# Two turns through the heads: weight slots that change contents in place of a ring of streamed pieces

## The chip, the core and the metric

The kernel runs on one core of a Trainium2 chip. The core has five engines with an instruction stream each: TensorE (PE; the profile shows its weight loads apart, as PEld), VectorE (DVE), ScalarE (ACT), GpSimd (POOL) and SyncE (SP), which here does nothing but issue DMAs. Sixteen DMA engines move data between DRAM and the on-chip memory SBUF. An engine takes its instructions in order, so an instruction that waits holds all behind it.

The metric is the time of one execution on the device, in microseconds: the median of three runs.

## The reference

Two independent models read their own inputs; their outputs are laid side by side. Part A is a dilated sliding-window attention. The change doesn't touch it except for copies that are made meanwhile. Part B is a recurrent memory transformer over 64 segments of 32 rows:

```python
# x: (1, 2048, 640), mem0: (1, 8, 640); 32 heads of 192; Wq, Wk, Wv: (640, 32, 192), Wo: (32, 192, 640)
mem = mem0
for s in range(64):
    h = concat([mem, x[:, 32 * s:32 * s + 32]], axis=1)          # 40 rows: 8 of memory, 32 of the segment
    q, k, v = h @ Wq, h @ Wk, h @ Wv                             # per head
    p = softmax(mask(q @ k.T * scale))
    o = (p @ v) @ Wo                                             # summed over the heads
    mem = o[:, :8]
    outs.append(o[:, 8:])
```

Each segment needs the memory of the one before, so the segments come one after the other, and each uses all four weights: 60 pieces of 384 KB for q, k and v, and 24 of 320 KB for the output, 31.5 MB in all. SBUF doesn't hold them all.

## The kernel before

**Part A** runs first (`part_a`, lines 24 to 265). Meanwhile SP loads weights of part B that fit beside it, then copies the weights that won't stay in SBUF to DRAM buffers in the layout in which they are fetched (`copy_streamed`), and issues the fourth x transpose (`turn_x(3)`) after these copies.

**A segment of part B.** The heads are taken in four groups of eight. Weight pieces have names (matrix, group, part): five for each group of q, k and v, six of output weights for each group. For each group a segment makes q, k and v (`project32`, matmuls of line 562 in PSUM tiles `acc`), moves them to SBUF and turns them, makes scores (line 626), a softmax, turns the probabilities (line 665), mixes the values (line 689, steps `mix` and `ot`) and multiplies with output weights: for the first three groups `project_out` (line 714, into Y), for the last one `project_last` (line 740). `close` adds the parts, writes the new memory into HX, the left operand of the next projections (line 748), and the output rows into XS (line 749).

The 40 rows of a segment are split: the main block of HX holds the 8 rows of memory and the first 24 x rows; the last 8 x rows of four segments stand together in a second block and are multiplied at once, ahead of their use (for the groups that table `RENEW` names for a segment; for q, one group at the end of each segment, step `ql`), and the results are kept in small blocks. The mixed values of these last 8 rows (the "late rows") are collected in DRAM (`late_o`, written by POOL's DMA, line 699) and multiplied with the output weights at the very end (`project_late`, line 859), four segments to a block.

**The order** is written out by hand as a list of steps, `ORDER` (`FIRST` for segment 0), and PE, DVE, ACT and SP follow it as written. The steps that matter here, in their order (a number is the group):

```python
q.0 k.0 k.1 q.1 v.0 q.2 k.2 v.1 q.3 k.3 out.0.0 v.2 out.0.1 v.3 PT.2 ve.2 ... out.1.1 out.2.0 out.2.1 part tx PT.3 mix.3 ot.3 last join ql close
```

`out.0.0` takes the first four output pieces of the group, `out.0.1` the other two. At `ve.2` SP is given the load of the next segment's x rows into XS (`load_x`, line 535), and at `tx` DVE turns these into HX (`turn_x`, line 531 from XS). The stores of the segment before (line 772, four of 7.5 KB) are given to SP at `tp.0`, `PT.0`, `tp.1` and `e.k3`.

**Weights.** 61 of the 84 pieces stay in SBUF (`wres_...`). The other 23, named in `STREAMED`, are fetched in each segment, in the order in which they are used, into a ring of seven slots (tile `t`, `fetch`, line 475): a fetch waits until PE has read the piece that was seven fetches earlier. SP issues them in the order of the program, and so runs seven slots ahead of PE. At the end, `project_late` goes through the output weights twice, for two blocks of rows at a time, with its resident pieces first and with the five streamed ones fetched again; the late rows are loaded into the dead q slots meanwhile (`load_late`).

Of the kernel before, what the change touches and what calls it, by code (L numbers as in the profile page):

```python
# [23 lines left out]
def part_a(ctx, tc, A_x, A_wqkv, A_wo, out, ident, emit_loads):  # L24
# [241 lines left out]
    with tc.manual_schedule(engines={mybir.EngineType.PE, mybir.EngineType.DVE, mybir.EngineType.Activation}):  # L266
# [4 lines left out]
        for b in range(-1, n_blk):  # L271
# [13 lines left out]
STREAMED = {"q": ((), (), (), ()), "k": ((1, 3), (1, 2), (0, 2), (1, 3)), "v": ((0, 1, 4), (2, 4), (0, 2, 4), (0, 2)),  # L285
            "o": (8, 12, 17, 19, 23)}
PARTS = {}
SLOT = 1536
# [18 lines left out]
SPREAD = "SSVV"  # L307
STORE_AT = ("tp.0", "PT.0", "tp.1", "e.k3")
LEAD_IN = 114
HEAD = 10  # L310
# [9 lines left out]
def part_b(ctx, tc, B_x, B_mem0, B_Wq, B_Wk, B_Wv, B_Wo, out, ident, n_seg, pre, nbuf, mid):  # L320
# [8 lines left out]

    def streamed(u):  # L330
        return u[1] in STREAMED["o"] if u[0] == "o" else u[2] in STREAMED[u[0]][u[1]]

# [15 lines left out]
    def quarter_cols(u):  # L348
        return 320 if u[0] == "o" else 384

    def load_quarters(dst, u, which):
        n = quarter_cols(u)
        for k, i in enumerate(which):
            to = dst[:, n * k:n * k + n]
            if u[0] == "o":
                src = unit_src(u)[:, i // 2].rearrange("p (b g c) -> p g b c", b=2, g=2)[:, i % 2]
                nc.sync.dma_start(to.rearrange("p (b c) -> p b c", b=2), src)
            else:
                nc.sync.dma_start(to, unit_src(u)[:, n * i:n * i + n])

    def quarter(w, u, i):

        n = quarter_cols(u)
        if isinstance(w, tuple):
            now = PARTS[u]
            v = w[0][:, n * i:n * i + n] if i < now else w[1][:, n * (i - now):n * (i - now) + n]
            return v.rearrange("p (b c) -> p b c", b=2) if u[0] == "o" else v
        if u[0] == "o":
            return w[:, 640 * (i // 2):640 * (i // 2) + 640].rearrange("p (b g c) -> p g b c", b=2, g=2)[:, i % 2]
        return w[:, n * i:n * i + n]  # L370

    def stream_cols(u):
        return quarter_cols(u) * PARTS.get(u, 4)

    def kept_cols(u):
        return quarter_cols(u) * (4 - PARTS[u]) if u in PARTS else unit_cols(u)

    copied = {}

    def copy_streamed():  # L380

        for m, g in need:
            for u in pieces(m, g):
                if u in PARTS:
                    copied[u] = dpool.tile([128, stream_cols(u)], BF16, name="wcopy_%s%d_%d" % u)[:]
                    load_quarters(copied[u], u, range(PARTS[u]))
                elif streamed(u):
                    copied[u] = dpool.tile([128, unit_cols(u)], BF16, name="wcopy_%s%d_%d" % u)[:]
                    nc.sync.dma_start(two_rows(copied[u], u), unit_src(u))

    need = [(m, g) for m, g in (("q", 0), ("k", 0), ("q", 1), ("k", 1), ("q", 2), ("k", 2), ("v", 0), ("v", 1), ("o", 0),
                                ("q", 3), ("k", 3), ("v", 2), ("o", 1), ("v", 3), ("o", 2), ("o", 3))]
    resident = []
    for m, g in need:
        resident += [u for u in pieces(m, g) if not streamed(u) or u in PARTS]
    res, wait = {}, set()

    def place_resident(pool, units):
        for u in units:
            res[u] = pool.tile([128, kept_cols(u)], BF16, name="wres_%s%d_%d" % u)[:]  # L400

    def load_resident(units):
        for u in units:
            if u in PARTS:
                load_quarters(res[u], u, range(PARTS[u], 4))
            else:
                nc.sync.dma_start(two_rows(res[u], u), unit_src(u))

    n_pre, used = 0, 0
    while n_pre < len(resident) and used < pre:  # L410
        used += 2 * kept_cols(resident[n_pre])
        n_pre += 1
# [28 lines left out]
    def emit_loads(turn_x):  # L441
        turn_x(1)
        load_resident(resident[:n_pre])
        turn_x(2)
        copy_streamed()
        return copy_windows
# [9 lines left out]
    wstream = pool("b_ws", bufs=nbuf)  # L456
    early = resident[n_pre:n_pre + 9]
# [13 lines left out]
    fetched = {}  # L471

    def fetch(u):
        t = wstream.tile([128, SLOT], BF16, tag="ws")
        nc.sync.dma_start(t[:, 0:stream_cols(u)], copied[u])
        return t[:, 0:stream_cols(u)]

# [7 lines left out]
    def get_unit(u):  # L485
        if u in wait:
            load_pending(u)
        if not streamed(u):
            return res[u]
        if u in fetched:  # L490
            w = fetched.pop(u)
        else:
            w = fetch(u)
            if pending:
                load_pending(pending[0])
        return (w, res[u]) if u in PARTS else w
# [155 lines left out]
    def put_p(s, g, t1, sm):  # L652
        i = s % 4
        if g == 0 and s:
# [14 lines left out]
    def spread_p(g, pt):  # L669
        PT = one.tile([128, 4, 2, L], BF16, tag="PT")  # L670
        if SPREAD[g] == "S":
# [34 lines left out]
    def project_out(Y, g, pairs=range(6)):  # L706
        for a in pairs:
            i = 6 * g + a
            w = get_unit(("o", i, 0))
            for r in range(2):  # L710
                c = 2 * a + r
                for gv in range(2):
                    t = 32 * (2 * r + gv)
                    nc.tensor.matmul(Y[t:t + 32].rearrange("p (b c) -> p b c", b=2),  # L714
                                     lhsT=OT[:, slot(c), 0:32], rhs=quarter(w, ("o", i, 0), 2 * r + gv),
                                     start=(i == 0), stop=(i == 17), tile_position=(0, t))
# [17 lines left out]
    def project_last(Y):  # L734
        for a in range(6):
            w = get_unit(("o", 18 + a, 0))
            for r in range(2):
                c = 2 * a + r
                for j in range(4):
                    nc.tensor.matmul(Y[32 * j:32 * j + 32], lhsT=OT[:, slot(c), 0:32],  # L740
                                     rhs=quarter(w, ("o", 18 + a, 0), 2 * r + j % 2)[:, j // 2],
# [16 lines left out]
    def segment(s):  # L758
# [9 lines left out]

        def step(name, *at):
            g = int(at[0][-1]) if at else None  # L770
            if ".".join((name,) + at) in STORE_AT and stores:
                nc.sync.dma_start(*stores.pop(0))
            if name in "qkv":
                project(name, g)
            elif name == "e":
                m = at[0][0]
                got["sb", m, g] = evacuate(m, got.pop((m, g)), [engine[c] for c in EVACUATE[at[0]]])
            elif name == "T":
# [3 lines left out]
                if m + at[0][1] == "k0" and s and keep:  # L782
# [17 lines left out]
            elif name == "PT":  # L800
                got["PT", g] = spread_p(g, got.pop(("p", g)))
            elif name == "ve":
                keep_values(g, got.pop(("v", g)))
                if g == 2:
                    load_x(s + 1)
            elif name == "mix":
                got["mix", g] = mix(g, got.pop(("PT", g)))
            elif name == "ot":
                keep_mix(s, g, got.pop(("mix", g)), [engine[c] for c in HEADS[g]])
            elif name == "out":  # L810
                g, half = int(at[0]), int(at[1])
                if "Y" not in got:
                    got["Y"] = ps_y.tile([128, 320], FP32, tag="y", name="Y")
                project_out(got["Y"], g, range(4 * half, 4 + 2 * half))
# [11 lines left out]
            elif name == "last":  # L826
                got["Z"] = bank()[:, 0:160]
                project_last(got["Z"])
# [10 lines left out]
    DEAD = [("q", g, dc) for g in range(4) for dc in range(5)]  # L839
# [4 lines left out]

    def project_late():

        O = [res[DEAD[b]].rearrange("p (g n c) -> p g n c", g=4, c=12) for b in range(16)]
        acc = [ps_acc.tile([128, 384], FP32, tag="acc", name=f"acc{n}") for n in range(3)]
        y = ps_y.tile([128, 320], FP32, tag="y")
        sums = [bank()[:] for _ in range(4)] + [acc[0][:], acc[1][:], acc[2][:], y[:]]  # L850
        head = [i for i in range(24) if not streamed(("o", i, 0))][:HEAD]
        tail = [i for i in range(24) if i not in head]

        def add(m, i, w, first, final):
            for r in range(2):
                c = (2 * i + r) % 12
                for gv in range(2):
                    for j in range(4):
# [3 lines left out]
                                         start=first and r == 0, stop=final and r == 1, tile_position=(0, 32 * j))  # L862
# [10 lines left out]
        for a, b in ((0, 1), (2, 3)):  # L873
            first = b == 1
            if first:
                load_late(range(8))
            for i in head:
# [110 lines left out]
```

## Time and profile before

| | us |
|---|---|
| median of three runs | 1859.13 (1856.05 to 1865.02) |
| the profiled execution, first to last instruction | 1879.4 |
| of it: start to line 748 of segment 0 | 207.8 |
| from there to line 748 of segment 62 | 1580.1 |
| last segment, up to the late products | 27.6 |
| late products and last stores | 63.9 |

The page of a profile gives the busy time of each engine over the span, the same in 40 slices of time, the DMA queues, the chain of work that ended last, and the costliest groups of instructions. "A <- B" behind an idle time means that B ended the wait of A. A line number is that of the kernel. PE's matmuls are pipelined and their ends modelled, so PE can be shown as busy while it runs below its peak. The names of DMAs are destination<-source: `t<-wcopy_v` is a fetch of a v piece into the ring, `wres_q<-in_B_Wq_dram` a load of a resident piece.

### The profile page before, as it was taken

How to read it: one execution, taken by the hardware profiler on the slowest of the kernel's cores; microseconds unless marked ns; L12 is line 12 of the kernel's file. 1: busy time of each engine (PE TensorE's matmuls, PEld its weight loads, DVE VectorE, ACT ScalarE, POOL GpSimd, SP SyncE). 2: the span in 40 equal slices, each digit the busy share in tenths (PEclk: the TensorE clock that was granted, in tenths of full speed). 3: DMA queues.
4: the chain of work that ended last, by engine and by line, in shares of the span. 5: the costliest groups of instructions: out<-in, count | busy, mean ns of one | idle time of the engine just before them, and what ended most of it. 6: DMA issues, size and time to landing. Idle time of an engine off the chain costs nothing.

```text
span 1879.4 us, 91426 instructions
## 1 busy us (share of the span) xinstructions
PE 1649.8 (88%) x39286; PEld 1048.1 (56%) x39286; DVE 1289.2 (69%) x3671; ACT 683.4 (36%) x1821; POOL 552.1 (29%) x1612
## 2 busy tenths in 40 slices
PE   8898888988888988988898889988888888889888
PEld 5565555555545555555555555555555555555568
DVE  4786776777666767767767767776677767777740
ACT  4454333333333333333333333333333333334320
POOL 3001322333322333323323323333333332333220
PEclk9999999999999999999999999999999999999999
DMA  9927999999999999999999999999999999999991
GB/s 327 319 72 258 368 356 335 362 365 362 350 340 328 351 330 368 355 360 352 357 341 367 345 345 361 366 364 339 354 355 354 348 338 356 348 355 371 331 373 36
DMA packets 277859, 627.63 MB, mean 334 GB/s; under 512 B 64116, under 2 KB 76898, under 8 KB 277452
## 3 DMA queue, kind: packets, MB, share of 16 engines
q1 hardware_dynamic: 267020, 610.59, 91.4%
q0 software_dynamic: 10336, 11.12, 1.7%
q8 instruction: 308, 5.05, 1.1%
q14 instruction: 99, 0.81, 0.1%
q10 hardware_dynamic: 96, 0.06, 0.0%
HBM read 607.47 MB, written 22.91 MB: 335 GB/s over the span
## 4 chain that ended last, share of the span: by engine, by line
PE 52%; DMA 25%; DVE 11%; issue 6%; ACT 4%; SPq 1%; POOL 0%; ACTq 0%; DVEq 0%; POOLq 0%
PE acc L562 27%; DMA t<-wcopy_v 19%; PE Y L714 6%; DMA t<-wcopy_k 4%; PE px L626 4%; PE px L689 3%; PE px L740 3%; PE pq L95 3%; PE px L859 2%; PE px L665 1%; DVE prod L151 1%; ACT OT L697 1%; DVE OT L697 1%; PE po L161 1%; ACT QT L721 1%
## 5 line engine op out<-in xcount | busy, mean ns | idle before, releaser
L562 PEld LDWEIGHTS <-HX 128*32 128x32 bf16 x19380 | 506.1, 97 | 373.4 <-issue 147.8
L562 PE MATMUL acc<-t,HX 128*32 128x384 bf16 x5812 | 432.5, 329 | 51.7 <-DMA t<-wcopy_v 34.8
L562 PE MATMUL acc<-wres_q,HX 128*32 128x384 bf16 x6460 | 328.4, 331 | 15.9 <-issue 14.0
L562 PE MATMUL acc<-wres_k,HX 128*32 128x384 bf16 x3876 | 271.3, 327 | 12.7 <-issue 10.6
L698 POOL COPY OL<-OT 128x96 bf16<-128x96 bf16 x256 | 159.4, 623 | 272.5 <-ACT OT L697 170.4
L562 PE MATMUL acc<-wres_v,HX 128*32 128x384 bf16 x3232 | 215.4, 328 | 7.9 <-issue 7.9
L697 DVE CAST OT<-px 128x240 bf16<-128x240 f32 x256 | 103.6, 405 | 168.4 <-PE px L689 153.0
L608 POOL COPY QT<-Lb 128x96 bf16<-128x96 bf16 x252 | 68.2, 271 | 482.5 <-PE px L626 482.1
L714 PE MATMUL Y<-wres_o,OT 128*32 128x320 bf16 x3840 | 193.0, 305 | 8.3 <-issue 8.3
L572 DVE STREAM_TRANSPOSE QT<-QT 128x384 bf16<-128x384 bf16 x256 | 146.6, 573 | 44.6 <-ACT QT L601 42.3
L601 ACT CAST KT<-acc 128x384 bf16<-128x384 f32 x192 | 92.4, 481 | 225.3 <-PE px L626 176.5
L697 ACT CAST OT<-px 128x240 bf16<-128x240 f32 x256 | 92.5, 361 | 217.5 <-PE px L689 123.7
L626 PE MATMUL px<-KT,QT 64*64 64x40 bf16 (+1 forms) x4096 | 138.7, 189 | 33.3 <-DVE KT L572 24.4
L615 ACT CAST Vst<-acc 128x384 bf16<-128x384 f32 x256 | 123.5, 483 | 118.1 <-PE px L689 94.0
L699 POOL DMA_DIRECT2D late_o<-OL x256 | 138.5, 541 | 77.0 <-POOL OL L698 60.8
L626 PEld LDWEIGHTS <-QT 64*64 64x64 bf16 (+1 forms) x4096 | 108.7, 109 | 90.8 <-issue 52.6
L632 DVE SCALAR_TENSOR_TENSOR px<-px,mask 128x160 f32<-128x160 f32 x256 | 82.7, 323 | 108.0 <-PE px L626 107.8
L714 PEld LDWEIGHTS <-OT 128*32 128x32 bf16 x4608 | 115.2, 97 | 62.4 <-issue 13.7
L572 DVE STREAM_TRANSPOSE KT<-KT 128x384 bf16<-128x384 bf16 x256 | 142.3, 556 | 3.3 <-ACT KT L601 1.7
L568 ACT CAST sb<-acc 128x384 bf16<-128x384 f32 x115 | 55.1, 479 | 236.3 <-PE acc L562 208.1
L689 PE MATMUL px<-PT,Vst 64*128 64x80 bf16 (+1 forms) x2048 | 123.5, 213 | 10.0 <-issue 6.3
L644 ACT ACTIVATE px<-px 128x160 f32<-128x160 f32 x256 | 74.2, 290 | 145.1 <-DVE px L643 137.0
(102 smaller groups left out, 2437.4 us busy)
## 6 DMA issues: line engine op xcount, KB each, us to landing
t<-wcopy_v SPq DMA_DIRECT2D x640, 384.0 KB, 5.7
t<-wcopy_k SPq DMA_DIRECT2D x512, 384.0 KB, 5.4
t<-wcopy_o SPq DMA_DIRECT2D x330, 320.0 KB, 5.9
wres_q<-in_B_Wq_dram SPq DMA_DIRECT2D x20, 384.0 KB, 7.8
late_o<-OL POOLq DMA_DIRECT2D x256, 24.0 KB, 5.2
wres_q<-late_o SPq DMA_DIRECT2D x16, 384.0 KB, 7.3
wres_o<-in_B_Wo_dram SPq DMA_DIRECT2D x19, 320.0 KB, 7.7
wres_k<-in_B_Wk_dram SPq DMA_DIRECT2D x12, 384.0 KB, 7.8
```

Source lines behind the costliest of these rows:

```text
L562: nc.tensor.matmul(ps[n][32 * j:32 * j + 32].rearrange("p (f n) -> p f n", n=32), lhsT=X[:, dc, :], rhs=columns(w, (m, g, dc), j), start=( ...
L572: nc.vector.transpose(t, t)
L601: copies[1](columns_of(m, 0, 32), ps[-1][:].rearrange("p (f n) -> p f n", n=32))
L615: S_(Vst[:], ps[-1][:])
L626: nc.tensor.matmul(Sps[64 * h:64 * h + 64, a, :], lhsT=QT[k0:k1, L * f:L * f + 64], rhs=KT[k0:k1, f, :], start=(outer == 0 and a == 0), st ...
L632: nc.vector.scalar_tensor_tensor(out=Sps, in0=Sps, scalar=scale, in1=mask[:].unsqueeze(1).to_broadcast([128, 4, L]), op0=ALU.mult, op1=ALU ...
L644: nc.scalar.activation(t1[:], t1[:], ACTF.Exp)
L689: nc.tensor.matmul(ps[r][lo:hi, 2 * L * k:2 * L * k + 2 * L], lhsT=V[64 * r:64 * r + 64, col:col + hi - lo], rhs=PT[64 * r:64 * r + 64, 2 ...
L697: copy(OT[:, 6 * r:6 * r + 6].rearrange("p c n -> p (c n)"), ps[r][:, 0:6 * L])
L698: nc.gpsimd.tensor_copy(OL[:, g % 2].rearrange("p n c -> p c n"), OT[:, :, 32:L])
L699: nc.gpsimd.dma_start(late_o[s // 4][:, g, s % 4], OL[:, g % 2].rearrange("p n c -> p (n c)"))
L714: nc.tensor.matmul(Y[t:t + 32].rearrange("p (b c) -> p b c", b=2), lhsT=OT[:, slot(c), 0:32], rhs=quarter(w, ("o", i, 0), 2 * r + gv), sta ...
```

## The change

The ring goes, and `STREAMED` with it. In its place:

- Odd segments take the groups in the order 3, 2, 1, 0 (`TURN`); even ones as before. The steps of `ORDER` now name positions, and the group is looked up. Tables of engines (`HEADS`, `SPREAD`, `EVACUATE`) go by position.
- Groups 0 and 3 of k, v and the output weights share slots (`SHARED`). When the group at position 0 has been used, its pieces are replaced by those of the other outer group (`change`, at k.0, v.0 and out.0.1), which is used at position 3 and, because the order turns, at position 0 of the next segment.
- One more slot holds pieces k1.4 and o17 in turn (`PAIR`): each is replaced by the other once it has been used.
- All of these are copied to DRAM during part A: 34 pieces (`copy_shared`) instead of 23.
- The load of XS remains at the step `ve` of position 2, and so follows the six output loads of `out.0.1` in SP's order.
- In the last segment the late rows, blocks 0 to 14, are loaded into the q slots as these fall free (at q of positions 0 to 2), and after v of position 1 the output pieces of group 0 go into slots of k and v (`load_outputs`), while the output pieces of group 3 stay. So all 24 are resident for `last` and for `project_late`, which takes one block of rows after the other through all weights.

```diff
+TURN = (0, 1, 2, 3), (3, 2, 1, 0)
+SHARED = (0, 3)
+PAIR = ("k", 1, 4), ("o", 17, 0)
...
+    def copy_shared():
+        for u in [u for g in SHARED[::-1] for m in "kvo" for u in pieces(m, g)] + list(PAIR):
+            copied[u] = dpool.tile([128, unit_cols(u)], BF16, name="wcopy_%s%d_%d" % u)[:]
+            nc.sync.dma_start(two_rows(copied[u], u), unit_src(u))
...
+    def replace(old, new):
+        slots[new] = slots.pop(old)
+        del res[old]
+        res[new] = slots[new][:, 0:unit_cols(new)]
+        nc.sync.dma_start(res[new], copied[new])
+
+    def change(m, g):
+        for old, new in zip(pieces(m, g), pieces(m, SHARED[0] + SHARED[1] - g)):
+            replace(old, new)
...
-    wstream = pool("b_ws", bufs=nbuf)
-    early = resident[n_pre:n_pre + 9]
+    early = resident[n_pre:n_pre + 16]
...
+        turn = TURN[s % 2]
+
         def step(name, *at):
-            g = int(at[0][-1]) if at else None
             if ".".join((name,) + at) in STORE_AT and stores:
                 nc.sync.dma_start(*stores.pop(0))
+            n = int(at[0][-1]) if at else None
+            g = turn[n] if at else None
             if name in "qkv":
                 project(name, g)
+                if name != "q" and n == 0:
+                    change(name, g)
+                if (name, g) == PAIR[0][0:2]:
+                    replace(*PAIR)
+                if s == 0 and n == 0 and name != "q":
+                    load_all("o", 1 if name == "k" else 2)
+                if last and name == "q" and n < 3:
+                    load_late(range(5 * n, 5 * n + 5))
+                if last and name == "v" and n == 1:
+                    load_outputs()
...
             elif name == "ve":
                 keep_values(g, got.pop(("v", g)))
-                if g == 2:
+                if n == 2:
                     load_x(s + 1)
...
+                project_out(got["Y"], g, range(4 * half, 4 + 2 * half), n == 0, n == 2)
+                if half and n == 0 and not last:
+                    change("o", g)
+                if half and g == PAIR[1][1] // 6 and not last:
+                    replace(*PAIR[::-1])
...
+    def load_outputs():
+        for old, new in zip(pieces("k", end[1]) + pieces("v", end[1]), pieces("o", end[3])):
+            replace(old, new)
...
     def project_late():
+        load_late((15,))
...
+        for m in range(4):
+            for i in range(24):
+                add(m, i)
+            store(m)
```

More of the change, by code (lines that the diff above doesn't have):

```diff
@@ L372, in stream_cols @@
[L372 to L376, printed above, removed]
-    copied = {}
[L380 to L389, printed above, removed]
@@ L487, in get_unit @@
             load_pending(u)
[L488 to L496, printed above, removed]
+        return res[u]
     mask = cpool.tile([128, L], BF16)
@@ L837, in segment @@
             step(*token.split("."))
-    DEAD = [("q", g, dc) for g in range(4) for dc in range(5)]
+    end = TURN[(n_seg - 1) % 2]
+    DEAD = [u for g in end for u in pieces("q", g)]
     def load_late(quads):
@@ L849, in project_late, with add @@
         y = ps_y.tile([128, 320], FP32, tag="y")
[L850 to L854, printed above, removed]
+        sums = [acc[0][:], acc[1][:], acc[2][:], y[:]] + [bank()[:] for _ in range(4)]
+        def add(m, i):
+            w = get_unit(("o", i, 0))
             for r in range(2):
```

128 lines of the change are left out of this document (35 added, 93 removed).

## The prediction

> **What bounds the kernel now.** I read the page first: busy times, DMA row, chain, DMA issues.
>
> ```profile
> span 1879.4 us, 91426 instructions
> ...
> PE 1649.8 (88%) x39286; PEld 1048.1 (56%) x39286; DVE 1289.2 (69%) x3671; ACT 683.4 (36%) x1821; POOL 552.1 (29%) x1612
> ...
> DMA  9927999999999999999999999999999999999991
> ...
> PE 52%; DMA 25%; DVE 11%; issue 6%; ACT 4%; SPq 1%; POOL 0%; ACTq 0%; DVEq 0%; POOLq 0%
> ...
> t<-wcopy_v SPq DMA_DIRECT2D x640, 384.0 KB, 5.7
> t<-wcopy_k SPq DMA_DIRECT2D x512, 384.0 KB, 5.4
> t<-wcopy_o SPq DMA_DIRECT2D x330, 320.0 KB, 5.9
> ```
>
> From a quarter of part A on, the DMA row stays at 9, and a quarter of the chain is DMA. The streamed pieces (`t`) are 10 v, 8 k and 5 o per segment: 18 x 393,216 + 5 x 327,680 bytes = 8.72 MB. Next the stages, from windows (columns: span; busy of PE, PEld, DVE, ACT, POOL; PE clock; DMA share; GB/s). The edges are line 748, which writes the recurrent memory into HX: once per segment, except the last.
>
> ```profile
> 0.00:170.00 170.00, 149.73 (x1971) 96.30 (x1972) 121.63 (x127) 81.65 (x159) 27.85 (x66) 0.99 0.75 236
> ...
> 207.80:1787.90 1580.10, 1388.08 (x34468) 864.30 (x34472) 1125.89 (x3426) 576.61 (x1595) 503.02 (x1488) 0.99 0.99 352
> 1787.90:1815.50 27.60, 22.82 (x551) 13.92 (x539) 17.46 (x52) 9.38 (x26) 9.31 (x26) 0.97 1.00 370
> 1815.50:1879.40 63.90, 55.37 (x1533) 52.65 (x1533) 1.97 (x4) 1.71 (x4) 1.32 (x3) 0.93 0.35 125
> ```
>
> 1580.1 us hold 62 segments: 25.49 us each. 8.72 MB at 352 GB/s are 24.8 us, and stores and x rows come on top: DMA sets the pace. What PE's waits say of the same stretch:
>
> ```profile
> PE acc L562 <- issue: 34.6, 49, 2.2
> PE acc L562 <- DMA t<-wcopy_v: 33.5, 62, 1.6
> ...
> PE px L689 <- issue: 10.0, 13, 1.3
> PE Y L714 <- issue: 8.7, 10, 2.8
> PE px L626 <- issue: 7.4, 14, 1.6
> PE px L740 <- issue: 5.3, 8, 1.3
> ...
> PE acc L562 <- DMA t<-wcopy_k: 3.9, 9, 0.7
> ...
> PE Y L714 <- DMA t<-wcopy_o: 1.1, 2, 0.6
> ```
>
> Weights: 38.5 us; "issue" (a sequencer with nothing to run): 66.0 us. The shortest segment of all shows how fast PE's own order can go (timeline):
>
> ```profile
> 1278.48 0.20 DVE L748 TENSOR_TENSOR HX<-Vst,KT 128x40 bf16<-128x40 f32 x1
> ...
> 1279.61 0.33 PE L562 MATMUL acc<-wres_k,HX 128*32 128x384 bf16 x4
> ...
> 1290.78 0.32 SPq L535 DMA_DIRECT2D XS<-xwindows  x1
> 1291.37 3.98 SPq L475 DMA_DIRECT2D t<-wcopy_o  x5
> ...
> 1292.12 0.73 PE L714 MATMUL Y<-wres_o,OT 128*32 128x320 bf16 x16
> ...
> 1293.69 0.46 PE L714 MATMUL Y<-wres_o,OT 128*32 128x320 bf16 x8
> ...
> 1298.01 0.35 DVE L531 STREAM_TRANSPOSE HX<-XS 128x160 bf16<-128x160 bf16 x1
> ...
> 1301.67 0.20 DVE L748 TENSOR_TENSOR HX<-Vst,KT 128x40 bf16<-128x40 f32 x1
> ```
>
> 23.2 us. Three marks count below: k's first piece is read 1.13 us after line 748 and done 0.33 later; the second part of the first output group is read at 15.2; line 531 turns the next segment's x rows (`tx`) at 19.5, and from there PT.3, mix.3, `last` and `close` take 3.66 to the next line 748.
>
> **The change, part by part.** *Traffic.* A segment now loads 5 k, 5 v and 6 o pieces (the other outer group's), plus o17 and k1.4 in turn: 11 x 393,216 + 7 x 327,680 = 6.62 MB, 24% less, 18.8 us at 352. The weight waits (38.5 us) go: a k piece is asked for at group 0 and used at group 3, some 10 us later.
>
> *What is late next: the x rows.* The load into XS stands behind `ve` of the third group in SP's order. Before, SP had run seven ring slots ahead and issued it at 12.3 us of the segment above, 7.2 ahead of `tx`. Now six o loads stand in front of it, and the last two wait until PE has read the first output group (15.2). So it is issued no earlier than that, as the last of a burst that began at k.0. How long it takes when something is queued and when not (line 535; and the lone load of the first rows):
>
> ```profile
> DMA to landing us min/median/max: 2.5/5.9/7.6
> XS<-xahead SPq DMA_DIRECT2D x1, 40.0 KB, 1.8
> ```
>
> Ahead of it go 5 k + 5 v pieces, o17 and 6 o: 10 x 393,216 + 7 x 327,680 = 6.23 MB, and about 0.12 MB of output rows, late rows and instructions (an estimate from 4 stores of 7.5 KB, three late_o of 24 KB and one fetch). At 352 GB/s: 18.0 us. Nothing breaks the burst: v is asked for near 6 us, while k still flows, and o near 13.5, while v does. So XS lands 1.13 + 0.33 + 1.8 + 18.0 = 21.3 us after line 748, 1.8 behind the 19.5 at which DVE wants it. DVE takes its work in order: behind `tx` it holds PT.3, and all of the segment's end waits for that. Segment = 21.3 + 3.66 = 24.9 us. Other waits ahead of `tx`, "issue" among them, lie under this one. The rate decides, so I bound it:
>
> ```profile
> 150.80:154.60 3.80, 3.80 (x34) 3.02 (x32) 3.77 (x5) 2.12 (x5) 0.54 (x1) 1.00 0.90 315
> ...
> 20.00:40.00 20.00, 19.33 (x352) 12.93 (x345) 12.54 (x14) 11.41 (x23) 2.30 (x3) 1.00 1.03 387
> 1815.00:1825.00 10.00, 9.42 (x204) 7.58 (x208) 0.00 (x0) 0.00 (x0) 1.82 (x4) 0.71 1.04 402
> ```
>
> 315 is three pieces just after the queue was empty, as it will be at each k.0; 387 and 402 are stages with hardly a store. The segment is 6.92 us + 6.35 MB / rate: 24.9 at 352, 23.3 at 387, 27.1 at 315. I take 352, the steady row, as stores, late rows and x rows keep their places. Sum: 62 x (24.9 - 25.49) = -37 us.
>
> *SP's other work.* The k loads wait for PE's k.0, and behind them on SP stand the pair's, v's, and the four stores of the segment before; nobody waits for the stores but the XS load, which comes later anyway. SP issues 18 pieces a segment instead of 23. Zero. The late rows go by POOL:
>
> ```profile
> late_o<-OL POOLq DMA_DIRECT2D x256, 24.0 KB, 5.2
> ```
>
> OL's two halves change by group, and at a turn the same group comes twice. Its first store has 5.2 us to land, and from the last group's mix of one segment to the first of the next lie more than 10 (`out`, which follows that mix, begins 13.6 us after line 748). Zero; without that cover POOL alone would wait, some us.
>
> *Order.* Groups renewed and the late q rows fall on other positions, as many as before; PE's work is the same. Zero, hidden by the 1.7 us that PE's order (23.2) has to spare below 24.9; if it is not, up to that much is already in the range.
>
> *Part A.* 34 pieces instead of 23 are copied to DRAM ahead of the fourth x transpose on SP: 12.5 against 8.7 MB.
>
> ```profile
> 60.00:80.00 20.00, 16.13 (x176) 9.75 (x180) 13.61 (x14) 8.24 (x17) 1.17 (x2) 0.91 1.00 300
> ...
> 88.02 7.12 SPq L49 DMA_TRANSPOSE xT<-in_A_x_dram  x1
> ...
> 107.08 1.30 PE L95 MATMUL pq<-xT,a_wq 128*32 128x512 bf16 x18
> ```
>
> 3.8 MB at 300 GB/s push it back 13 us, to land near 110; its first reader, the 46th group of line 95, stands at 107.1. +3 us (0 to 6). Residents: 110,592 bytes a partition are loaded early in both.
>
> *Segment 0.* 32 pieces behind the early ones, where there were more: 0.
>
> *Last segment.* SP issues there 15 blocks of late rows, 5 k, 5 v, o17 and the six pieces of output group 0, which `last` needs: 25 x 393,216 + 7 x 327,680 = 12.1 MB, at 370 GB/s 32.8 us, from 1.1 us on and with 1.8 of latency: 35.7 us, against 27.6 from line 748 to the late products now (the row above). +8 us.
>
> *Late products.* No fetches among them.
>
> ```profile
> 1825.00:1835.00 10.00, 8.19 (x238) 7.60 (x232) 0.00 (x0) 0.00 (x0) 0.00 (x0) 1.00 0.74 272
> 1835.00:1845.00 10.00, 10.00 (x304) 10.00 (x296) 0.00 (x0) 0.00 (x0) 0.00 (x0) 1.00 0.23 69
> 1870.00:1875.00 5.00, 2.76 (x81) 2.46 (x73) 0.49 (x1) 0.43 (x1) 0.00 (x0) 1.00 0.12 34
> ```
>
> 1536 products at 304 in 10 us are 50.5 us; with the tail after PE's last (6.6 us) 57 instead of 63.9. I take -6, as the 402 row has the clock at 0.71 while they begin.
>
> Sum against the profiled execution: 1879.4 - 37 + 3 + 8 - 6 = 1847. The median of the runs shown, 1859.13, is 0.989 of 1879.4, so the same share: 1827 us, 1.7% faster.
>
> A rule to weigh: at 1835 PE runs full while DMA is quiet, at 1825 it idles 1.8 us without a wait; I take the "issue" idle time for instruction fetches that queue behind weights, and count none of it in the quiet end and start of a segment. [...]
>
> **The rivals.** *(a) XS lands in time.* Above 387 GB/s the rows come before 19.5, and PE's order sets 23.2: 62 x -2.29 = -142, with the +5 of start and end 1742, times 0.989 = 1723. For it: the 387 and 402 rows, and less traffic in all. Against: eight tenths of the segment are as full as now. [...]
> *(b) The burst runs slowly (slower than before).* The queue is empty at each k.0 and restarts; at 315 throughout, 27.1 us: +100 + 5, 1984, times 0.989 = 1962. It decides from 340 GB/s down, where the segment is 25.6. For it: the 315 row. Against: the steady row averages over just such mixes.
> *(c) The change does not reach the path.* If only the 38.5 us of weight waits went and "issue" stayed, 1879.4 - 38.5 + 5 = 1846, times 0.989 = 1826: the same time by another way, with `tx` on time.
>
> **How the numbers follow.** Less than 0.5% (9 us) can hardly be told from no change. 24.3 to 25.2 us a segment, with (c): 0.46, around 1827 (1790 to 1846); (a), 23.2 to 24.2: 0.24; between 25.2 and 25.6, no change: 0.10; (b): 0.20. Faster 0.70, same 0.10, slower 0.20. The range leaves out the lowest tenth of (a)'s side and the far half of (b): 1740 to 1880.
>
> **What would show it.** Line 531 (HX from XS) waits for DMA XS, 1 to 2 us in nearly every segment: right; waits of line 562 for weights near zero. No such wait and segments near 23.3: (a). Waits for wres_k, wres_v or wres_o in the steady segments: the loads are late in a way I excluded. PE waiting for xT near 107, and for wres_o in the last segment, test the ends. A DMA rate other than 352 from k.0 to `tx` makes the time wrong, by 0.05 us a segment for each GB/s.

## The result and the profile after

The changed kernel takes 2141.29 us (median of four runs, 2131.94 to 2151.24), the kernel before, run beside it, 1862.08: a ratio of 1.150, with a 95% interval of 1.144 to 1.156. The change makes the kernel 15% slower.

In the changed kernel the lines have moved: the projections are line 518 (before 562), the x rows' load 491 (535), `tx` and the other transposes 487 (531), the reload of a slot 375, the end of `close` 705 (748), the stores 730 (772), `PT` 632, the mix 645, `last` 697. From its page: span, busy times, the rows of the clock and of DMA, the chain by engine and by line, and the group of `tx`.

```profile
span 2129.8 us, 90744 instructions
...
PE 1733.2 (81%) x39286; PEld 1110.6 (52%) x39286; DVE 1294.1 (61%) x3687; ACT 674.9 (32%) x1805; POOL 545.5 (26%) x1612
...
PEclk9999989999899999999999898989999999899989
DMA  9929766667666677666677666766667666677670
...
PE 54%; DMA 22%; DVE 15%; issue 4%; ACT 3%; SPq 2%; POOL 1%; DVEq 0%; ACTq 0%; POOLq 0%
PE acc L518 28%; DMA XS<-xwindows 17%; PE px L582 5%; PE px L697 5%; PE px L645 5%; PE pq L95 3%; PE Y L670 2%; PE px L621 2%; DVE QT L528 2%; SPq L375 2%; DVE KT L528 1%; DMA wres_k<-wcopy_o 1%; DVE PT L632 1%; DVE sb L528 1%; PE px L841 1%
...
L487 DVE STREAM_TRANSPOSE HX<-XS 128x160 bf16<-128x160 bf16 x65 | 23.0, 354 | 246.2 <-DMA XS<-xwindows 246.2
```

The DMA row, nines before, is now sixes and sevens, and yet a DMA is what DVE waits for: the x rows, 246.2 us, and 17% of the chain. From the waits of PE, and of SP:

```profile
PE px L645 <- DVE PT L632: 239.5, 62, 7.0
...
PE px L582 <- issue: 11.2, 25, 1.3
...
PE pq L95 <- DMA xT<-in_A_x_dram: 7.8, 2, 4.9
...
PE acc L518 <- DMA wres_v<-wcopy_v: 4.5, 5, 2.6
```

```profile
SPq L375 <- DMA wres_v<-wcopy_v: 112.0, 180, 2.3
SPq L730 <- DMA wres_v<-wcopy_v: 69.7, 91, 2.0
```

PE stands behind DVE's `PT` for 239.5 us, 62 times, so 3.9 us in every segment: `PT.3` is queued on DVE behind `tx`. And SP itself waits for transfers: its reloads of slots and even its stores (line 730) wait until value pieces have landed, whose contents neither needs. Where a segment ends, by the line that writes the memory:

```profile
L705 DVE TENSOR_TENSOR HX<-Vst,KT x63: 199/199/201, 213.6 to 2035.2; 128x40 bf16<-128x40 f32 x63
```

62 segments in 1821.6 us are 29.38 each, against 25.49 before: +241 us. The first segment's end comes 5.8 us later than before (213.6 against 207.8). Windows of the end and of one steady segment (columns as in the windows of before):

```profile
2070.00:2129.80 59.80, 53.36 (x1584) 52.92 (x1584) 3.08 (x8) 1.85 (x5) 3.21 (x6) 0.98 0.08 23
```

```profile
1002.12:1005.62 3.50, 3.50 (x56) 1.94 (x52) 1.68 (x5) 0.48 (x1) 1.27 (x6) 0.59 0.02 7
1005.62:1010.62 5.00, 4.89 (x124) 2.91 (x112) 3.62 (x9) 1.98 (x5) 1.37 (x6) 1.00 0.81 258
1010.62:1016.62 6.00, 5.48 (x136) 3.50 (x140) 4.86 (x18) 3.19 (x10) 1.16 (x5) 1.00 1.02 397
1016.62:1021.62 5.00, 4.89 (x138) 3.19 (x130) 3.98 (x14) 1.91 (x6) 1.81 (x5) 1.00 0.92 304
1021.62:1030.68 9.06, 4.93 (x132) 3.45 (x128) 4.00 (x14) 1.86 (x6) 2.57 (x6) 0.90 0.55 182
```

Read it with what SP issues in it (timeline: start, length, number):

```profile
1005.36 2.47 SPq L375 DMA_DIRECT2D wres_k<-wcopy_k  x5
1007.93 0.38 SPq L375 DMA_DIRECT2D wres_k<-wcopy_o  x1
1009.17 3.78 SPq L375 DMA_DIRECT2D wres_v<-wcopy_v  x5
1013.60 3.15 SPq L730 DMA_DIRECT2D out_dram<-XS  x4
1017.33 4.66 SPq L375 DMA_DIRECT2D wres_o<-wcopy_o  x6
1022.11 0.36 SPq L491 DMA_DIRECT2D XS<-xwindows  x1
```

The queue is empty for 3.5 us, runs at 258 GB/s while it fills, at 397 while values flow, and at 304 when the output pieces are issued one by one over 4.7 us. The rows, issued last, are turned only at 1026.6. And in the first 3.5 us PE, which works without a break there, has a granted clock of 0.59.

Means over 58 steady segments, put together from the trace's records, in us after line 705 (the prediction's value in brackets): first k product 2.08 (1.13), first reload issued 2.60 (1.46), its first packet 3.56, last packet of the rows 24.42, `tx` 24.99 (21.3), next line 705 at 29.36 (24.9).

### The profile page after: what moved, and what is told of

The parts are those of the page before. It is cut to its first block, busy times and chain, and to the rows that moved or that the text cites. A ratio compares the mean times of both kernels' runs of the same rounds, so it can differ in the third digit from the quotient of the medians.

```text
span 2129.8 us, 90744 instructions
## 1 busy us (share of the span) xinstructions
PE 1733.2 (81%) x39286; PEld 1110.6 (52%) x39286; DVE 1294.1 (61%) x3687; ACT 674.9 (32%) x1805; POOL 545.5 (26%) x1612
## 4 chain that ended last, share of the span: by engine, by line
PE 54%; DMA 22%; DVE 15%; issue 4%; ACT 3%; SPq 2%; POOL 1%; DVEq 0%; ACTq 0%; POOLq 0%
PE acc L518 28%; DMA XS<-xwindows 17%; PE px L582 5%; PE px L697 5%; PE px L645 5%; PE pq L95 3%; PE Y L670 2%; PE px L621 2%; DVE QT L528 2%; SPq L375 2%; DVE KT L528 1%; DMA wres_k<-wcopy_o 1%; DVE PT L632 1%; DVE sb L528 1%; PE px L841 1%
## 5 line engine op out<-in xcount | busy, mean ns | idle before, releaser
L518 PEld LDWEIGHTS <-HX 128*32 128x32 bf16 x19380 | 515.0, 102 | 334.3 <-issue 100.4
L518 PE MATMUL acc<-wres_q,HX 128*32 128x384 bf16 x6460 | 378.4, 379 | 6.8 <-issue 3.3
L518 PE MATMUL acc<-wres_v,HX 128*32 128x384 bf16 x6460 | 319.6, 329 | 17.1 <-ACT KT L557 9.4
L645 PE MATMUL px<-PT,Vst 64*128 64x80 bf16 (+1 forms) x2048 | 127.7, 220 | 247.5 <-DVE PT L632 239.5
L518 PE MATMUL acc<-wres_k,HX 128*32 128x384 bf16 x6460 | 303.3, 330 | 4.5 <-issue 2.3
L645 PEld LDWEIGHTS <-Vst 64*128 64x128 bf16 (+1 forms) x2048 | 70.8, 101 | 338.8 <-issue 292.4
L670 PE MATMUL Y<-wres_o,OT 128*32 128x320 bf16 x4352 | 200.0, 303 | 10.4 <-issue 4.5
L487 DVE STREAM_TRANSPOSE HX<-XS 128x160 bf16<-128x160 bf16 x65 | 23.0, 354 | 246.2 <-DMA XS<-xwindows 246.2
L524 ACT CAST sb<-acc 128x384 bf16<-128x384 f32 x99 | 47.4, 479 | 290.0 <-PE acc L518 265.0
L548 POOL COPY Lb<-sb 128x96 bf16<-128x96 bf16 x453 | 104.3, 268 | 132.1 <-DVE sb L528 132.1
```

What stands on the lines that cost most here:

```text
L518: nc.tensor.matmul(ps[n][32 * j:32 * j + 32].rearrange("p (f n) -> p f n", n=32), lhsT=X[:, dc, :], rhs=columns(w, (m, g, dc), j), start=( ...
L548: nc.gpsimd.tensor_copy(late[m, g, t][:], rows(t))
L645: nc.tensor.matmul(ps[r][lo:hi, 2 * L * k:2 * L * k + 2 * L], lhsT=V[64 * r:64 * r + 64, col:col + hi - lo], rhs=PT[64 * r:64 * r + 64, 2 ...
```

## The experiments

All were run beside the kernel before, which took 1865 to 1870 us in each set (medians). Experiments one, three and four are one execution each, five, six, nine and ten two, the others four or more; the four of the changed kernel spread over 19 us. Experiments three and six add work; all compute the whole output. The first four share one question: is the loss the wait for the rows and what hangs on it (theory X), or is the burst of reloads too slow, so that whatever stands last in it will be late (theory Q)?

**One: the rows' load moved ahead of the output pieces.**

```diff
 elif name == "ve":
     keep_values(g, got.pop(("v", g)))
-    if n == 2:
-        load_x(s + 1)
...
     g = turn[n]
+    if half and n == 0:
+        load_x(s + 1)
     project_out(got["Y"], ...)
```

> The changed kernel with the load of the x rows given to SP just ahead of the six output loads instead of behind them; the four stores stay where they are. Theory X (the rows' place behind the output loads makes DVE wait, PE falls idle, and its clock is halved after the idle time): DVE's wait for XS falls from 246 us to under 60, the mean clock rises from 0.915 to 0.96 or more, a segment takes 25 to 26 us instead of 29.4, the time is near 1890 us. As the rows then wait for the fourth store to land, the output loads start later and some wait for them in the last group appears. Rival Q (the queue is too slow, whatever comes first): another wait, of PE for output weights, takes the place, and the time stays above 2080.

Measured: 2103.52 us. The wait for the rows is gone and another has its place (waits of PE and of SP):

```profile
PE px L697 <- DMA wres_o<-wcopy_o: 168.2, 250, 3.4
```

```profile
SPq L491 <- DMA out_dram<-XS: 254.6, 76, 5.5
```

`last` now waits for output pieces. XS is also the source of the four stores; SP holds the rows' load until these have landed, 254.6 us in all, with the output pieces queued behind it: the first of them is issued 18.9 us after line 705 in the mean, where it was 15.0. The time is in theory Q's range, but this doesn't show Q's cause: SP's wait for the stores, which theory X names as a side effect, makes the output pieces late as well.

**Two: rows' load and stores both early** (`load_x` in the step `tp` of the first group).

```diff
-    STORE_AT = ("tp.0", "PT.0", "tp.1", "e.k3")
+    STORE_AT = ("k.1", "e.k0", "T.k0", "q.1")
...
     got["p", g] = turn_p(g)
+    if n == 0:
+        load_x(s + 1)
```

> The changed kernel with the four stores given to SP between the k and the v loads, and the x rows' load at the first turn of the probabilities (step tp of position 0), ahead of the output loads. Theory X: no wait for XS, none of half a microsecond for weights, clock 0.97 or more, segments of 23.5 to 24.3 us, so 62 x 23.9 + 308 = 1790 us (1745 to 1815), below the kernel before. Rival Q: the burst at 304 GB/s ends no earlier, so output weights are late for the last group, and the time stays above 2000. Rival C (the clock is throttled by denser work, not by the wait): the wait goes, but the clock stays near 0.92 and segments near 25.5.

Measured: 1863.91 us, 0.997 (0.993 to 1.001) of before. All of the loss is undone, with segments of 25.1 us, no wait of DVE for the rows and a mean clock of 0.978, but nothing is gained. That is theory X's cause with a worse time than the 1790 us it gave; theory Q's burst, too late wherever the rows stand, would have kept the time above 2000.

```profile
L705 DVE TENSOR_TENSOR HX<-Vst,KT x63: 199/201/202, 214.7 to 1771.1; 128x40 bf16<-128x40 f32 x63
```

PE still waits for weights:

```profile
PE px L697 <- DMA wres_o<-wcopy_o: 23.7, 51, 1.9
PE acc L518 <- DMA wres_v<-wcopy_v: 21.7, 28, 2.1
```

So the places of one 40 KB load and of the four small stores that it waits for, moved together, decide 277 us, and behind them a burst that is still late for PE shows.

**Three: PE kept busy in the wait, with narrow products.**

```diff
 elif name == "mix":
+    if n == 3 and s and not last:
+        warm = bank()
+        for _ in range(130):
+            nc.tensor.matmul(warm[:, 0:8], lhsT=ident, rhs=ident[:, 0:8], start=True, stop=True)
```

> The changed kernel with 130 small products (8 columns, 27 ns each, 3.5 us) put into PE's order ahead of the last mix of each segment, where PE now idles; their results are not used, and nothing else changes. Theory X: the wait of DVE for XS stays near 3.9 us, but PE is no longer idle, the clock rises from 0.915 to 0.97 or more, and the stretches behind the wait and up to the next k go back from 4.47 and 2.08 us towards 3.66 and 1.13: a segment is up to 1.7 us shorter, 2020 us in all (1990 to 2060). Rival C: more work on PE, clock 0.915 or below, the time unchanged or longer than 2130.

Measured: 2155.96 us, in rival C's range, mean granted clock 0.908 against 0.915 (the rows of the cores, of the changed kernel and of this one, PE's timeline and PE's waits):

```profile
core 0: 2129.8 us, clock 0.915
```

```profile
core 0: 2154.1 us, clock 0.908
```

```profile
1013.56 3.56 PE L780 MATMUL px<-ident 128*128 128x8 bf16 x130
```

```profile
PE px L645 <- DVE PT L632: 17.1, 28, 2.2
```

PE waits only 17.1 us for `PT` now, and the mean clock is as low all the same. By this run alone the low clock would not be PE's standing idle; experiment six tells the two apart.

**Four: the rows' load issued by POOL.**

```diff
-    nc.sync.dma_start(XS[:], ...)
+    (nc.gpsimd if s > 1 else nc.sync).dma_start(XS[:], ...)
```

> The changed kernel with the x rows' load issued by POOL instead of SP, nothing else changed. Theory X (the rows wait because SP issues them behind six output loads and its queue is served in order): they land earlier than the output loads, the wait of DVE for XS falls from 246 to under 80 us, segments of 24.5 to 25.5 us, 1830 to 1900 us. Rival Q (the DMA engines are full, whichever queue): landing and wait as now, time above 2080.

Measured: 2056.99 us, between the two theories.

```profile
DVE HX L487 <- DMA XS<-xwindows: 183.2, 62, 5.4
```

Out of SP's order DVE still waits 183.2 us for the rows: a quarter of the wait went. But POOL hardly issues the load sooner: it stands before it for 190 us in all, and issues it 18.3 us after line 705 in the mean of 58 segments, where SP did at 19.2. So the run doesn't show what a load issued ahead of the output pieces would do. What it does show is that a queue of its own doesn't make the load quick: from issue to landing it takes 5.5 us (median; SP's in the changed kernel 5.2 to its last packet).

**Five: the four stores made one.** In the trace of the changed kernel SP's transfers signal their landing on eight semaphores in turn (1643 transfers, 204 to 206 on each semaphore; 1630 have that of the one eight before), and at 1537 of them SP waits for the semaphore that it is about to use, so each of these waits for the landing of the one eight places before; four small stores take half of these places.

```diff
-    stores.extend((out2[SEG * s:SEG * s + SEG - M, ...], Ysb[32 * j + M:32 * j + SEG]) for j in range(4))
+    if s:
+        rows = out2[SEG * s - M:SEG * s + SEG - M, Dm:2 * Dm].rearrange("n (j c) -> j n c", j=4)
+        stores.append((rows, Ysb))
+    else:
+        ...                                        # segment 0 as before
```

> The changed kernel with the segment's four stores of 24 x 160 output values made into one of 128 x 160 (its first eight rows in each block land on rows that the late products write again at the end; nothing is left out). Theory L: the burst is slow because SP's transfers each wait for the landing of the one eight places before, and the four small stores hold four of the eight places, so the output pieces of the first group go out one by one as value pieces land. With one store they go out at once behind the first output products: the burst ends 1 to 1.9 us earlier, the wait for the rows falls from 246 us to some 150 (120 to 190), and the time is 2050 us (2020 to 2085). Theory R: the burst runs at this rate whatever the order of issue: wait 235 to 250, time 2125 to 2150.

Measured: 2095.65 us, 46 us less, between the two theories:

```profile
DVE HX L487 <- DMA XS<-xwindows: 210.1, 63, 5.0
```

In the segment shown the output pieces leave SP in 2.96 us instead of 4.66 (3.5 instead of 4.1 in the mean):

```profile
1003.59 2.96 SPq L375 DMA_DIRECT2D wres_o<-wcopy_o  x6
```

In the mean segment the first of them still is issued only at 14.8 us and the last at 17.8, behind the first group's output products, the last of which end at 16.8; the values' last packet comes at 16.6. First reload's first packet to the rows' last: 20.3 us, where it was 20.9.

**Six: wide products in the wait.**

```diff
+    if n == 3 and s and not last:
+        warm = bank()
+        for _ in range(14):
+            nc.tensor.matmul(warm[:, 0:384], lhsT=ident, rhs=LV[turn[0]][:], start=True, stop=True)
```

> The changed kernel with 14 products of 384 columns into a spare bank ahead of the last mix of each segment, 3.8 us of PE work at full clock in the wait for the rows (they add work and leave nothing out). Theory C: the clock is halved because PE stands idle for more than 3 us behind the rows' transpose; with PE at work there, the mean granted clock goes from 0.915 to above 0.97, the stretch from the rows' transpose to the end of the segment from 4.5 us to 3.7, the way from there to the first key product from 2.1 us to 1.2, and the time falls by 62 x 1.5 = 95 us to 2045 (2010 to 2090). Theory N: the halved clock has another cause, or costs nothing on the path: clock 0.90 to 0.93, time 2130 to 2160.

Measured: 2048.5 us, as theory C has it:

```profile
core 0: 2054.8 us, clock 0.974
```

```profile
L705 DVE TENSOR_TENSOR HX<-Vst,KT x63: 199/200/202, 217.1 to 1959.1; 128x40 bf16<-128x40 f32 x63
```

```profile
DVE HX L487 <- DMA XS<-xwindows: 248.9, 63, 6.2
```

The rows are as late as ever, 248.9 us, and the segment is 28.10 us instead of 29.38. From `tx` to the end it is 3.64 us (4.37), and the first k product comes at 1.34 (2.08). That is 79 us for 62 segments, the rest of the 93 lies in the differences of the ends and of the executions. In the changed kernel's clock records the halved stretches (granted clock 0.5) last 3.41 or 6.83 us (64 of 67), mostly one to a segment. In the 3.41 us ahead of one, PE stands idle for 2.9 us in the mean, and in experiment one, whose clock is 0.921, for 2.2 us in several waits, the longest of them 1.0 us in the median. In the changed kernel's steady segments, with the full clock cut into windows of 3.41 us back from each halved stretch, none of the 339 windows with under 1.2 us of idle time was followed by a halved clock, and each of the 58 with over 1.5 us was. In experiment three 130 products of 8 columns ran for 3.56 us without a gap, and the mean clock stayed at 0.908; with 14 of 384 columns, 2.5 us, it is 0.974.

**Seven: experiment two with the one store.**

> Experiment two (the rows loaded at the first group's probabilities, the stores early) with the four stores made into one. Theory L: there too the stores' places held back the output pieces that the last products wait for; those waits (45 us of output and value pieces) halve, and the time goes from 1864 to 1840 us (1825 to 1850). Theory R: the rate sets it, and the time stays at 1855 to 1870.

Measured: 1831.19 us, 0.984 (0.978 to 0.990) of before, in theory L's range, segments of 24.4 us: 1.6% faster than the kernel before. PE's wait of 23.7 us is down to a third:

```profile
PE px L697 <- DMA wres_o<-wcopy_o: 8.2, 17, 1.5
```

**Eight: the first group's keys, values and output products ahead of the rest** (on experiment seven).

```diff
-    q.0 e.q0 T.q0 k.0 k.1 e.k0 T.k0 q.1 S.0 sb.0 e.k1 e.q1 mx.0 sub.0 v.0 T.q1 ve.0 T.k1 q.2 S.1 send.0
+    k.0 q.0 e.k0 e.q0 T.k0 T.q0 v.0 ve.0 k.1 q.1 S.0 sb.0 e.k1 e.q1 mx.0 sub.0 T.q1 T.k1 q.2 S.1 send.0
...
-    PT.1 mx.2 sub.2 k.3 T.q3 send.2 out.0.0 e.k3 v.2 out.0.1 mix.1 T.k3
+    PT.1 mx.2 sub.2 out.0.0 out.0.1 k.3 T.q3 send.2 e.k3 v.2 mix.1 T.k3
```

> The one before, with the order of work changed: the first group's key and value products ahead of everything but the first query products, and its output products ahead of the fourth group's key products, so that each exchange starts earlier (keys by 1 us, values by 3, output weights by 2). If the start of the exchange is what is late: the waits for weights vanish, PE is busy for all but 2 us of a segment, 24.0 us each, and the time is 1790 us (1765 to 1820). Rival: the chain of scores, softmax and mix of the groups now starts later and takes the waits' place: 1850 to 1900.

Measured: 1858.45 us, slower than experiment seven, as the rival has it. PE's longest wait is now for the turned keys of the scores:

```profile
PE px L582 <- DVE KT L528: 78.1, 63, 1.3
```

**Nine: two transfers for the five or six pieces of a group.** The pieces of a shared group lie in two tiles, in SBUF and in DRAM, of three and two or three and three.

```diff
 def change(m, g):
-    for old, new in zip(pieces(m, g), pieces(m, SHARED[0] + SHARED[1] - g)):
-        replace(old, new)
+    for old, new in zip(halves(m, g), halves(m, SHARED[0] + SHARED[1] - g)):
+        ...                                        # the names change places
+        whole[new[0]] = whole.pop(old[0])
+        nc.sync.dma_start(whole[new[0]], halved[new[0]])
```

> The changed kernel with the pieces of a shared group moved by two transfers (three and two pieces, or three and three) where there were five or six; same bytes, same packets, nothing left out. Theory O: the exchange runs at 304 GB/s because only five or six transfers of 0.33 to 0.39 MB are under way, issued 0.47 us apart and held by the eight places; with a whole half in each the rate goes to 350 GB/s or more, the burst of 6.55 MB shrinks from 21.5 us to 18.7 and the segment from 29.4 us to 26.7: 1975 us (1930 to 2030). Theory M: the rate is what the engines do with these packets however they are issued: 300 to 310 GB/s, and the first transfer of each group starts up to 0.7 us later, since it waits for three pieces' products: 2140 us (2110 to 2180).

Measured: 2076.49 us, between the theories. The same stretch of a segment, 5.0 to 8.0 us (changed kernel) and 5.5 to 8.5 us (experiment nine) after line 705 or its like, where keys flow:

```profile
1007.12:1010.12 3.00, 2.92 (x80) 1.84 (x76) 2.20 (x7) 1.00 (x3) 1.37 (x6) 1.00 0.96 318
```

```profile
1020.53:1023.53 3.00, 2.94 (x76) 2.05 (x79) 2.27 (x8) 1.54 (x5) 0.10 (x1) 1.00 1.02 410
```

The same bytes go at 410 GB/s instead of 318 (395 instead of 317 in the mean of 58 segments) when a transfer holds 0.8 to 1.2 MB instead of 0.39, with a DMA share near 1 in both (0.96 and 1.02). So here, where the changed kernel has 5.9 transfers of SP under way (mean over the stretch shown), larger ones go faster; while values flow, with 7.9 under way, it has 397. What is gained there is partly lost at the start: the first packet comes 0.56 us later (4.12 against 3.56), since the transfer waits for three pieces' products. The 65 us of the whole run aren't shown to be the size alone, as two transfers also take fewer of SP's eight places.

**Ten: the first output products sooner** (on experiment five; the second half of experiment eight's diff).

> The one-store kernel (2095.7 us) with the first group's output products ahead of the fourth group's key products instead of around the fourth group's value work. Theory G: between the landing of the last value piece, some 15.5 us into the segment, and the issue of the output pieces, behind the last output product at 16.5, the queue runs dry, and the rate falls from 405 GB/s to 263; with the output products 2 us sooner the queue stays full: the rate in that stretch stays above 350, the wait for the rows falls from 210 us to some 110, and the time is 2000 us (1960 to 2045). Rival: the rate falls there for another reason (the transfers of each group start slowly, wherever they stand), the burst ends less than 0.5 us earlier: 2065 to 2100 us.

Measured: 2015.75 us, in the range of theory G, with a wait for the rows of 156.9 us where 110 were expected:

```profile
DVE HX L487 <- DMA XS<-xwindows: 156.9, 62, 6.8
```

One segment's stretch from 14.5 to 19.5 us, where the changed kernel had 304 GB/s (means of 58 segments: 355, experiment five 306, the changed kernel 275):

```profile
1007.71:1012.71 5.00, 4.57 (x124) 2.87 (x113) 4.41 (x15) 1.55 (x5) 2.38 (x6) 1.00 1.02 385
```

In experiment five the queue ran short there, but not dry as theory G supposed: the first output piece's first packet came at 15.3 us, ahead of the values' last (16.6).

**Eleven: experiment seven with the two transfers.**

> Experiment seven (1831 us) with the two transfers a group. If Theory O holds: weights that land sooner have little left to give, since PE waited 8 us for output weights there; the restart of each segment gains some: 1822 us (1808 to 1835). If the coarser transfers are late instead: the fourth group's first product waits for a whole half, and 1835 to 1870.

Measured: 1830.61 us, 0.981 (0.976 to 0.986) of before: no difference from experiment seven. Where the exchange is no longer what PE waits for, a faster one gives nothing.

**Twelve: nine and ten together** (one store, output products sooner, two transfers; the rows' load where the change has it).

> The changed kernel with the one store, the output products sooner and the two transfers a group, the rows' load left where the change has it (behind the output pieces). Theory S: the three causes of the slow burst are what made the change slow. In the 2022.5 us profile of experiment ten the values have landed 15 us into the segment; with halves the keys and values land 0.5 us sooner still and the output pieces and rows (2.0 MB) run at 370 GB/s behind output products that end at 14.3: rows there by 20.5 to 21.5, wait for the rows below 60 us, and since PE then stands idle for less than 1.5 us the clock comes back by itself, above 0.97: segment 24.6 to 25.4 us, time 1855 us (1830 to 1895). Rival, the gains merely add: experiment nine's 65 us off experiment ten's 2016 us, with a wait of 90 us or more and the clock still near 0.94: 1925 to 1975 us.

Measured: 1979.0 us, where the sum of the single gains would be 1950. That is 4 us above the rival's range and far from theory S's; the gains merely add, and not all of them.

```profile
DVE HX L512 <- DMA XS<-xwindows: 129.6, 61, 4.5
```

First packet to the rows' last packet is now 18.7 us, near the 18.0 predicted. But it starts at 3.73, and PE still stands still for 1.9 us in the mean, and the clock is halved in 40 of the 58 steady segments (mean 0.944): a segment takes 27.0 us. With the rows behind the reloads the segment isn't saved by a faster burst.

## Why the prediction was wrong

Forecast: 1.7% faster. Result: 15.0% slower, outside the range, on the side of rival (b). Against the sum for the profiled execution, 1847 us, the span of 2129.8 is 283 us more. 62 segments of 29.38 instead of 24.9 make 278 of them. A misreading on which nothing rests: the DMA row of before isn't at nine from a quarter of part A on; its third and fourth slices, 94 to 188 us, have 2 and 7.

- **The x rows late at `tx`: right as a mechanism.** Line 487 waits for XS in nearly every segment, and the prediction's "1 to 2 us" was 3.9. Weight waits near zero: right, 4.5 us for values and 1.5 for keys.
- **"Nothing breaks the burst", 18.0 us at 352 GB/s: the step that failed.** The burst took 20.9 us (+2.9 us a segment): 304 GB/s by the prediction's own 6.35 MB. The trace has 6.66 MB in that time, part of k1.4 behind the rows among them, so 319 GB/s; the rate makes up some 2 of the 2.9 us and the bytes the rest. The burst doesn't run unbroken: the queue starts empty and is short while keys flow (258 GB/s), and it runs short again between values and output pieces (304, down to four transfers under way). I took 352 from a stretch in which the ring kept SP's transfers under way all the time, 6.2 in the mean; the row of 315, from a queue just restarted, was the nearer one, and I gave it 0.20. Three causes were shown, here one added to the other: the places that the stores take (20.3 us without them), output products too late to ask for the next pieces (19.5), transfers too small for a short queue (18.7). "SP's other work … zero" fell with it: the stores cost 46 us by their four places, not by their bytes, of which the one store has no fewer.
- **The clock: not in the prediction at all.** I priced the stretch from `tx` on at 3.66 us and the way to the first k product at 1.13, both from a segment at full clock (1.00), in which PE stood still for 1.6 of 23.2 us, at most 0.6 at a time. Behind the wait of 3.9 us the clock is halved (0.59 in the first 3.5 us of the segment shown): 4.37 and 2.08. Experiment six puts it at 1.3 us a segment. It lengthens the segment but not the wait: a later first k product starts the next burst later (2.60 against 1.82), but DVE comes later to `tx` as well, and the wait for the rows is the same with and without it (246.2 and 248.9 us).
- **The terms of the start of a segment:** first reload issued at 2.60 instead of 1.46, +1.14, of which 0.78 is the clock (1.82 in experiment six); from issue to first packet and from last packet to `tx` 0.96 + 0.57 instead of 1.8, -0.27; burst +2.86; end +0.71. Together 24.9 + 4.4 = 29.3, the measured segment.
- **Part A +3, last segment +8, late products -6:** measured +5.8, some +7 (34.8 us from line 705 to the late products), and -4.1 (59.8 against 63.9). Right to 4 us in all.
- **Rival (b)** had the restart from an empty queue, part of the cause, and "it decides from 340 GB/s down", but priced it at 27.1 us, without the clock. **(a)** is what experiment two allows (no wait for the rows), and still it ends at 25.1 us a segment, not 23.2. Late output pieces and values are 0.7 us of these 1.9; 23.2 was the shortest segment of all, and what else keeps the mean from it was not tested. 24% less traffic gained nothing until the stores had become one. **(c)** fell: "issue" went from 66 us to some 30, with 11.2 as its largest row, and that gained nothing. That this idle time is instruction fetches, as the prediction took it, fits the trace of before: the 82 such waits over 0.3 us end 1.4 us (median; eight of ten 0.8 to 1.6) after an instruction packet has come, where moments picked at random are 2.5 us behind one.
- **"Order … zero"** weighed PE's work alone. Where the first group's output products stand also sets when the output pieces are asked for, and moving them was worth 80 us (experiment ten against five).

## What to carry to other kernels

A transfer that is needed at a fixed moment must not be queued behind a burst that is sized to fill the time up to it: here a load of 40 KB in the wrong place, with the stores ahead of it, cost 277 us. When a ring that always has transfers under way is replaced by exchanges that start from an empty queue, take the rate from a restarted queue (here 258 to 318 GB/s while keys flow, against 352), and count the places and sizes of the transfers, not the bytes alone. And price new waits of PE with the clock that follows them: here it was halved behind each window of 3.41 us with over 1.5 us of idle time (changed kernel), and in experiment one behind 2.2 us in several waits.

## What the runs showed of the hardware

- A granted clock of 0.5 for 3.41 or 6.83 us behind the waits of 3.9 us (mean), a mean of 0.915. With 130 gapless products of 8 columns in the wait (27 ns each by 219.1 us for 8060) the mean was 0.908, with 14 of 384 columns (2.5 us) 0.974. Several shorter waits, the longest 1.0 us in the median and 2.2 us together in the 3.41 us ahead, went before it too (experiment one, 0.921).
- In the segments shown, keys at 318 GB/s in transfers of 0.39 MB with 5.9 of SP's transfers under way in the mean, at 410 GB/s in transfers of about 1 MB (experiment nine), the DMA share near 1.0 in both (0.96 and 1.02): here that share didn't tell the rate.
- A store or load issued by SP waited up to 2.0 and 2.3 us for the landing of value pieces that it has nothing to do with, eight places ahead in its order (69.7 us in 91 waits of the stores, 112.0 in 180 of the reloads, in each for the transfer eight before, with the same semaphore). That the eight semaphores are the cause was read from the trace's semaphores and SP's waits; experiment five, which leaves one store of the four, agrees, and puts them at 46 us.
